# TensorE's program of a decode kernel: steps 16 to 127 as a hardware loop, with queries staged per group

## The chip, the cores and the metric

One core of one Trainium2 chip runs the kernel. The metric is the device time in microseconds (us) of one execution. A profiled execution gives a trace as well; its span is some 2 us shorter than the device time (1290.62 and 1292.84 us for the kernel before). Runs of one kernel agree within 0.7 us, so differences of 1 us can be told apart, although the verdict "same" covers everything within 2%. In the names of the profile PE is TensorE and PEld its weight loads, DVE is VectorE, ACT is ScalarE and SP is SyncE; a q behind a name stands for that engine's sequencer.

## The reference

A decode step for four sequences: layer norm, attention of one query token per sequence over a cache of 8192 keys and values in 32 heads, a residual, a second layer norm, a gated feed-forward block, a residual. Cut to what matters:

```python
B, Sq, D = 4, 1, 512
H, Sk, Dh = 32, 8192, 128
k_cache, v_cache: (B, H, Sk, Dh) bfloat16      # 268 MB each
q = (layernorm(x) @ wq) -> (B, H, 1, Dh)
p = softmax(q k^T * Dh**-0.5);  o = p v;  h = x + o @ wo
out = h + (sigmoid(g) * u) @ w_down,  g, u = layernorm(h) @ w_gate, w_up    # F = 1792
```

The caches are read once, and little is computed on each byte: the kernel is a stream out of HBM with some work alongside.

## The kernel before

A small scheduler collects the operations of every engine with their dependencies, counts semaphore values and writes each engine's program out in full. There are 128 steps, one per (sequence, head). K and V are loaded two heads at a time, 4 MB a load, into a ring of four slots. In each step DVE transposes the head's K in four pieces, TensorE computes 16 score matmuls, and ten steps later 16 matmuls with V. Softmax work is done per group of eight steps.

```python
GS, LAG, NS = 8, 10, 4                       # group size, lag of V behind K, ring slots

def emit(self, name, e):                     # one engine's program
    seen = {}
    for op in self.ops[name]:
        need = {}
        ...                                  # highest semaphore values that op's dependencies have
        for k, (v, s) in need.items():
            e.wait_ge(s, v)                  # a wait on a constant
            seen[k] = v
        ins = op.fn(e)
        if op.inc:
            ins.then_inc(op.sem, 1)
...
def dve_T(s):                                # K of step s, transposed by DVE in four pieces
    ...
    q = HT // 4
    for i in range(4):
        def f(e, i=i):
            return e.transpose(kT[:, buf, i * q:(i + 1) * q].bitcast(U32),
                               ringv(src)[:, base + i * q:base + (i + 1) * q].bitcast(U32))
        op = P("dve", f, [dma_of[it][0], sc_of.get(s - 2)])
        yield
...
def pe_score(s):                             # 16 matmuls; every step's queries have an address of their own
    t, u, g = s // 2, s % 2, s // GS
    hh = 4 * u + t % 4
    def f(e):
        mm = None
        for v in range(4):
            l0 = LQ0 + (t * 4 + v) * 32 - 4 * hh
            for j in range(4):
                rhs = ...
                mm = e.matmul(bS[g % 2][32 * j:32 * (j + 1), :], Lq[:, l0:l0 + 32], rhs, ...)
        return mm
```

The loads are issued by SyncE, each when its slot's last reader is done: a K slot after the DVE transposes, a V slot after the V matmuls on TensorE. After the last V come the weights of the output projection and of the feed-forward block (w_gate, w_up, then w_down in three pieces).

## Time and profile before

| | before |
|---|---|
| device time, median | 1293.15 us (1293.1 to 1293.17) |
| bytes from HBM | 550.77 MB, 427 GB/s over the span |
| data queue's share of the 16 DMA engines' time | 99.4% |
| busy: TensorE, DVE | 39%, 49% |
| instruction packets on queue 8 | 38, of 16 KB each |

From the page of the kernel before: the busy times; the span in 40 slices (DMA busy in tenths, and GB/s); the DMA queues (packets, MB, share of 16 engines); the chain that ended last, by engine and by line.

```profile
PE 499.5 (39%) x4851; PEld 189.0 (15%) x4851; DVE 637.6 (49%) x659; ACT 74.4 (6%) x134; POOL 10.6 (1%) x22
...
DMA  9999999999999999999999999999999999999997
GB/s 406 433 426 436 427 434 430 431 432 429 433 429 431 432 431 431 430 431 432 430 433 428 432 427 436 432 427 434 428 434 426 434 431 430 434 428 434 428 432 305
...
q1 hardware_dynamic: 20384, 550.78, 99.4%
q8 instruction: 38, 0.62, 0.2%
q14 instruction: 7, 0.06, 0.0%
...
DMA 85%; PE 12%; DVE 2%; issue 0%; SPq 0%; DVEq 0%
DMA ring<-in_A_v_cache_dram 78%; PE PS L436 7%; PE PS L412 4%; DMA ring<-in_B_w_up_dram 3%; DMA ring<-in_A_k_cache_dram 2%; DVE kT L394 1%; DMA ring<-in_A_wq_dram 1%; PE PS L467 0%; PE PS L323 0%; PE PS L631 0%; DVE Lq L367 0%; DVE ring L340 0%; PE PS L350 0%; PE PS L645 0%; DVE mx L450 0%
```

Every slice but the last has the DMA engines busy; the last one has the tail. Queue 1 carries the data, queues 8 and 14 carry instructions; the text calls the reading of one such instruction packet a fetch. No compute engine comes near full use, so outside the tail no saving of compute can pay directly.

The last pieces of the chain of waits, in order of time (start, duration, what):

```profile
1234.61 3.63 PE PS L436 x32
...
1238.68 43.65 DMA ring<-in_B_w_up_dram
...
1282.38 3.54 PE PS L631 x56
```

The kernel ends 8.28 us after the load of w_up lands at 1282.34 us. Whatever moves that landing moves the kernel.

Three rows of the timeline in the steady state (start, duration, engine, line, operation, in brackets what ended the idle time before it):

```profile
610.28 0.33 SPq L249 DMA_DIRECT2D ring<-in_A_k_cache_dram  x1
...
615.03 0.33 SPq L249 DMA_DIRECT2D ring<-in_A_v_cache_dram  x1
...
619.50 5.75 DVE L394 STREAM_TRANSPOSE kT<-ring 128x1024 uint32<-128x1024 uint32 x5 [2.70 <-DMA ring<-in_A_k_cache_dram]
```

A K slot is issued again at 610.3 us and a V slot at 615.0 us, while earlier loads are still to land.

One more reading was made from the trace. A load runs on 16 DMA engines, and each adds one to the load's semaphore when its share has landed (the trace has 16 such updates for each load). The 16 times of one load show how far the engines are apart. They are not labelled with the engine, so only their sorted order is known. For four loads (K loads except the last row; time of the first of the 16, then the sorted delays behind it, all in us):

```
before, first at    delays of the 16 shares
   90.0   0 .15 .23 .24 .28 .30 .34 .36 .37 .43 .50 .85 1.28 1.73 1.83 1.86
  478.6   0 .13 .19 .25 .38 .39 .82 1.55 1.77 2.10 3.22 3.33 3.35 3.37 3.39 3.90
  944.9   0 .06 .07 .26 .30 .61 .95 3.90 4.55 4.83 4.84 4.86 5.43 6.25 6.37 6.40
 1274.6   0 .01 .02 .16 .31 .51 .89 4.75 5.94 6.20 6.30 6.80 7.56 7.70 7.71 7.76   (w_up)
```

The fastest engine delivers a 4 MB load every 9.71 us from beginning to end. I call the last number of a row the lag.

### The profile page before, as it was taken

The numbers are of one execution on the slowest core, as the hardware profiler recorded it, in microseconds if no ns is written. First come the engines' busy times: TensorE is split into PE (matmuls) and PEld (weight loads), VectorE is DVE, ScalarE is ACT, GpSimd is POOL, SyncE is SP. The second block draws the span as 40 slices with busy tenths as digits, with TensorE's granted clock in tenths as the row PEclk, the third lists the DMA queues.
The fourth block names the chain that finished last, engine by engine and source line by source line (L and its number), as shares of the span: only waits on it lengthen the run. The fifth ranks groups of instructions, "written<-read, shape, count | busy, mean of one in ns | idle before, by whom it ended". The sixth has DMA issues, their size and how long they took to land.

```text
span 1290.6 us, 10784 instructions
## 1 busy us (share of the span) xinstructions
PE 499.5 (39%) x4851; PEld 189.0 (15%) x4851; DVE 637.6 (49%) x659; ACT 74.4 (6%) x134; POOL 10.6 (1%) x22
## 2 busy tenths in 40 slices
PE   2444334334234244333334343342343443443445
PEld 1011111111011011111111111110110111111114
DVE  5974644535545545535536445445445446355300
ACT  2010100001010010100101000010100101000011
POOL 3000000000000000000000000000000000000000
PEclk8556566565565665565665666665655656655665
DMA  9999999999999999999999999999999999999997
GB/s 406 433 426 436 427 434 430 431 432 429 433 429 431 432 431 431 430 431 432 430 433 428 432 427 436 432 427 434 428 434 426 434 431 430 434 428 434 428 432 305
DMA packets 20437, 551.46 MB, mean 427 GB/s; under 512 B 2212, under 2 KB 2216, under 8 KB 3624
## 3 DMA queue, kind: packets, MB, share of 16 engines
q1 hardware_dynamic: 20384, 550.78, 99.4%
q8 instruction: 38, 0.62, 0.2%
q14 instruction: 7, 0.06, 0.0%
q10 hardware_dynamic: 8, 0.00, 0.0%
HBM read 550.77 MB, written 0.00 MB: 427 GB/s over the span
## 4 chain that ended last, share of the span: by engine, by line
DMA 85%; PE 12%; DVE 2%; issue 0%; SPq 0%; DVEq 0%
DMA ring<-in_A_v_cache_dram 78%; PE PS L436 7%; PE PS L412 4%; DMA ring<-in_B_w_up_dram 3%; DMA ring<-in_A_k_cache_dram 2%; DVE kT L394 1%; DMA ring<-in_A_wq_dram 1%; PE PS L467 0%; PE PS L323 0%; PE PS L631 0%; DVE Lq L367 0%; DVE ring L340 0%; PE PS L350 0%; PE PS L645 0%; DVE mx L450 0%
## 5 line engine op out<-in xcount | busy, mean ns | idle before, releaser
L394 DVE STREAM_TRANSPOSE kT<-ring 128x1024 uint32<-128x1024 uint32 x512 | 588.1, 1209 | 480.7 <-DMA ring<-in_A_k_cache_dram 480.7
L412 PE MATMUL PS<-kT,Lq 128*32 128x512 bf16 x2048 | 242.7, 621 | 565.9 <-DVE kT L394 565.6
L436 PE MATMUL PS<-ring,PTz 128*32 128x512 bf16 x2048 | 216.6, 569 | 201.9 <-DMA ring<-in_A_v_cache_dram 201.9
L412 PEld LDWEIGHTS PS<-kT,Lq 128*32 128x32 bf16 x2048 | 70.2, 135 | 699.6 <-DVE kT L394 601.0
L436 PEld LDWEIGHTS PS<-ring,PTz 128*32 128x32 bf16 x2048 | 66.6, 128 | 320.0 <-DMA ring<-in_A_v_cache_dram 191.5
L497 DVE STREAM_TRANSPOSE Et<-Ep 128x512 bf16<-128x512 bf16 x16 | 11.4, 711 | 95.7 <-ACT Ep L493 95.7
L471 ACT ACTIVATE negm<-PS 128x1 f32<-128x1 f32 x16 | 2.7, 171 | 674.1 <-PE PS L467 674.1
L506 ACT ACTIVATE PTz<-Et 64x512 bf16<-64x512 bf16 x32 | 34.0, 1061 | 12.8 <-DVE Et L497 12.4
L534 ACT ACTIVATE A_sb<-PS 32x32 bf16<-32x32 f32 x16 | 3.8, 235 | 485.5 <-PE PS L532 485.5
L511 DVE TENSOR_SCALAR Zs<-PS,rinv 128x512 f32<-128x512 f32 x16 | 11.6, 723 | 27.7 <-PE PS L436 27.7
L518 PE MATMUL PS<-SelZ,Zs 128*128 128x8 f32 x128 | 18.4, 270 | 0.9 <-DVE Zs L511 0.9
L518 PEld LDWEIGHTS PS<-SelZ,Zs 128*128 128x128 f32 x128 | 16.9, 206 | 10.4 <-issue 8.6
L450 DVE TENSOR_REDUCE mx<-PS 128x1 f32<-128x512 f32 x16 | 10.5, 657 | 4.2 <-PE PS L412 4.1
L473 ACT ACTIVATE E_sb<-PS,negm 128x512 bf16<-128x512 f32 x16 | 11.0, 687 | 0.5
L493 ACT ACTIVATE Ep<-PS 128x512 bf16<-128x512 f32 x16 | 9.6, 597 | 10.4 <-PE PS L489 10.4
L478 PEld LDWEIGHTS PS<-sig,Gsum 128*128 128x128 f32 x32 | 7.8, 304 | 13.0 <-issue 13.0
L478 PE MATMUL PS<-sig,Gsum 128*128 128x1 f32 x32 | 9.2, 357 | 0.0
L467 PEld LDWEIGHTS PS<-onesf,rowx 1*128 1x128 f32 x32 | 6.6, 254 | 12.6 <-issue 12.6
L631 PE MATMUL PS<-hnT,ring 128*128 128x4 bf16 x112 | 7.0, 199 | 2.9 <-DMA ring<-in_B_w_gate_dram 2.0
L467 PE MATMUL PS<-onesf,rowx 1*128 1x1 f32 x32 | 7.9, 314 | 0.0
L524 DVE TENSOR_TENSOR OD<-PS,SelD 128x32 bf16<-128x32 f32 x16 | 2.5, 156 | 10.3 <-PE PS L518 10.3
L340 DVE CAST ring<-PS 128x512 bf16<-128x512 f32 x4 | 2.5, 682 | 10.0 <-PE PS L323 10.0
(85 smaller groups left out, 100.3 us busy)
## 6 DMA issues: line engine op xcount, KB each, us to landing
ring<-in_A_k_cache_dram SPq DMA_DIRECT2D x64, 4096.0 KB, 29.7
ring<-in_A_v_cache_dram SPq DMA_DIRECT2D x64, 4096.0 KB, 33.9
ring<-in_A_wq_dram SPq DMA_DIRECT2D x1, 4096.0 KB, 12.4
kT<-in_A_wo_dram SPq DMA_DIRECT2D x1, 2560.0 KB, 40.5
ring<-in_B_w_gate_dram SPq DMA_DIRECT2D x1, 1792.0 KB, 39.7
ring<-in_B_w_up_dram SPq DMA_DIRECT2D x1, 1792.0 KB, 43.7
kT<-in_A_wo_dram SPq DMA_DIRECT2D x1, 1536.0 KB, 43.7
ring<-in_B_w_down_dram SPq DMA_DIRECT2D x1, 896.0 KB, 37.2
```

The costliest lines, as they stand in the source:

```text
L394: return e.transpose(kT[:, buf, i * q:(i + 1) * q].bitcast(U32), ringv(src)[:, base + i * q:base + (i + 1) * q].bitcast(U32))
L412: mm = e.matmul(bS[g % 2][32 * j:32 * (j + 1), :], Lq[:, l0:l0 + 32], rhs, start=(s % GS == 0 and v == 0), stop=(s % GS == GS - 1 and v == 3),
L436: mm = e.matmul(bO[g % 2][32 * rq:32 * (rq + 1), :], PTz[:, g % 2, l0:l0 + 32], ringv(slot)[:, r0 * 128:(r0 + 4) * 128], start=(s % GS == ...
L450: mx_of[g] = P("dve", lambda e: e.tensor_reduce(mx[:, :], bS[g % 2][:, :], AX.X, ALU.max), [sc_of[g * GS + GS - 1], p1_of.get(g - 1)])
L467: p2_of[g] = P("pe", lambda e: e.matmul(bX[:, 0:1], rowx[0:1, :], onesf[0:1, 0:1], start=True, stop=True), [d2b_of[g], c_ones])
L473: exp_of[g] = P("act", lambda e: e.activation(E_sb[:, :], bS[g % 2][:, :], ACT.Exp, bias=negm[:, 0:1], scale=SCALE, accum_out=sig[:, 0:1]) ...
L478: L_of[g] = P("pe", lambda e: e.matmul(bX[:, 0:1], Gsum[:, :], sig[:, 0:1], start=True, stop=True), [exp_of[g], a1_of[g], d_g])
L493: epc_of[g] = P("act", lambda e: e.activation(Ep[:, :], bP[0][:, :], ACT.Copy), [pt_of[g], et_of.get(g - 1)])
L497: et_of[g] = P("dve", lambda e: e.transpose(Et[:, :], Ep[:, :]), [epc_of[g]] + list(ptc_of.get(g - 1, ())))
L506: return e.activation(dst, src, ACT.Copy)
L511: z_of[g] = P("dve", lambda e: e.tensor_scalar(Zs[:, :], bO[g % 2][:, :], rinv[:, g % 2:g % 2 + 1], None, op0=ALU.mult), [pv_of[g * GS + G ...
L518: mm = e.matmul(bP[1][:, 0:8], Zs[:, 128 * r:128 * (r + 1)], SelZ[:, r, :], start=(r == 0), stop=(r == 3))
```

## The change

TensorE's program for steps 16 to 127 becomes seven passes of a body of 16 steps. For this, everything that differed between passes has to become the same: ScalarE copies the queries of each group to a fixed address ahead of the group (`Lqg`), one product is put at a fixed PSUM row, waits compare with a register that is raised in each pass, and dummy operations make the counts of the first pass equal to those of the others. The evident intent is a smaller program; the arithmetic is the same. The diff, cut to its core:

```diff
+L0, LB = 16, 16
...
     def emit(self, name, e):
+        turns = self.turns(name) if name == "pe" else []
         for op in self.ops[name]:
+            if name == "pe" and op.turn is not None:
+                if op is turns[0][0]:
+                    self.emit_loop(name, e, turns, seen)
+                continue
...
+    def emit_loop(self, name, e, turns, seen):
+        ...
+        with e.Fori(0, len(turns)) as i:
+            for same, ds in zip(zip(*turns), fixed):
+                ...
+                    e.wait_ge(s, i * self.step[k] + base)
+                ins = same[0].fn(e)
+                if same[0].inc:
+                    ins.then_inc(same[0].sem, 1)
...
-        Lq = SB("Lq", [128, 32 + NT2 * 128], BF16)
+        Lq = SB("Lq", [128, NT2 * 16], BF16)
+        Lqg = SB("Lqg", [128, 2, LQ0 + 516], BF16)
...
+        def chain_lq(g):
+            lqg_of[g] = P("act", lambda e: e.activation(
+                Lqg[:, g % 2, LQ0:LQ0 + 512].rearrange("p (i a) -> p i a", a=32)[:, :, 0:4],
+                Lq[:, 64 * g:64 * g + 64].rearrange("p (i a) -> p i a", a=4), ACT.Copy),
+                [sc_of.get((g - 2) * GS + GS - 1), zlg] + ...)
...
-                    l0 = LQ0 + (t * 4 + v) * 32 - 4 * hh
+                    l0 = LQ0 + ((t % 4) * 4 + v) * 32 - 4 * hh
...
-            a_of[g] = P("pe", lambda e: e.matmul(bP[1][r0:r0 + 32, 16:48], OD[:, :], SelS[:, :], start=True, stop=True,
-                                                 tile_position=(0, r0)), [otc_of[g], d_sels, ac_of.get(g - 1)])
+            a_of[g] = P("pe", lambda e: e.matmul(bP[1][0:32, 16:48], OD[:, :], SelS[:, :], start=True, stop=True,
+                                                 tile_position=(0, 0)), [otc_of[g], d_sels, ac_of.get(g - 1)])
...
+        def blank(s, base, eng):             # dummy operations on ACT and DVE for equal counts
...
         for s in range(NST + LAG + 4):
+            prog.turn = (s - L0) // LB if L0 <= s < NST else None
```

More of the change, by code (lines that the diff above doesn't have):

```diff
@@ L17 @@
 NS = 4
+L0, LB = 16, 16
 class _Op:
-    __slots__ = ("eng", "fn", "deps", "inc", "val", "sem", "amount")
+    __slots__ = ("eng", "fn", "deps", "inc", "val", "sem", "turn")
     def __init__(self, eng, fn, deps):
@@ L36, in __init__ @@
         self.ops = {e: [] for e in self.ENGS}
+        self.turn = None
     def add(self, eng, fn, deps=(), sem=None, val=0):
@@ L40, in add @@
         op.sem, op.val = sem, val
+        op.turn = self.turn
         self.ops[eng].append(op)
@@ L49, in resolve @@
                         d.inc = True
+        self.step = {}
         for e in self.ENGS:
+            turns = self.turns(e)
+            for same in zip(*turns):
+                if any(op.inc for op in same):
+                    for op in same:
+                        op.inc = True
             n = 0
@@ L55, in resolve, with turns, needs @@
                     op.sem, op.val = sems[e], n
+            if turns:
+                assert len({len(t) for t in turns}) == 1
+                self.step[id(sems[e])] = sum(op.inc for op in turns[0])
+    def turns(self, e):
+        by = {}
+        for op in self.ops[e]:
+            if op.turn is not None:
+                by.setdefault(op.turn, []).append(op)
+        return [by[k] for k in sorted(by)]
+    @staticmethod
+    def needs(name, op, but=()):
+        need = {}
+        for d in op.deps:
+            if d in but or d.eng == name == "pe":
+                continue
+            k = id(d.sem)
+            if d.val > need.get(k, (0, None))[0]:
+                need[k] = (d.val, d.sem)
+        return need
     def emit(self, name, e):
         seen = {}
+        turns = self.turns(name) if name == "pe" else []
         for op in self.ops[name]:
-            need = {}
-            for d in op.deps:
-                if d.eng == name == "pe":
-                    continue
-                k = id(d.sem)
-                if d.val > seen.get(k, 0) and d.val > need.get(k, (0, None))[0]:
-                    need[k] = (d.val, d.sem)
-            for k, (v, s) in need.items():
-                e.wait_ge(s, v)
-                seen[k] = v
+            if name == "pe" and op.turn is not None:
+                if op is turns[0][0]:
+                    self.emit_loop(name, e, turns, seen)
+                continue
+            for k, (v, s) in self.needs(name, op).items():
+                if v > seen.get(k, 0):
+                    e.wait_ge(s, v)
+                    seen[k] = v
             ins = op.fn(e)
@@ L72, in emit @@
                 ins.then_inc(op.sem, 1)
+    def emit_loop(self, name, e, turns, seen):
+        first = {}
+        fixed = [set(same[0].deps).intersection(*(op.deps for op in same[1:])) for same in zip(*turns)]
+        for op, ds in zip(turns[0], fixed):
+            for k, (v, s) in self.needs(name, op, set(op.deps) - ds).items():
+                if v > seen.get(k, 0):
+                    e.wait_ge(s, v)
+                    seen[k] = v
+        with e.Fori(0, len(turns)) as i:
+            for same, ds in zip(zip(*turns), fixed):
+                need = [self.needs(name, op, ds) for op in same]
+                for k in sorted({k for n in need for k in n}, key=lambda k: [k in n for n in need]):
+                    vals = [(t, n[k][0]) for t, n in enumerate(need) if k in n]
+                    s = next(n[k][1] for n in need if k in n)
+                    if k not in self.step:
+                        self.step[k] = (vals[-1][1] - vals[0][1]) // (vals[-1][0] - vals[0][0])
+                    base = {v - t * self.step[k] for t, v in vals}
+                    assert len(base) == 1, (vals, self.step[k])
+                    base = base.pop()
+                    if k in first and base <= first[k]:
+                        continue
+                    first[k] = base
+                    e.wait_ge(s, i * self.step[k] + base)
+                ins = same[0].fn(e)
+                if same[0].inc:
+                    ins.then_inc(same[0].sem, 1)
+        for k, base in first.items():
+            seen[k] = base + (len(turns) - 1) * self.step[k]
 def bass_sequential_preLN__mha_block_cached__glu_gated_glu__decode_kernel(
@@ L133, in bass_sequential_preLN__mha_block_cached__glu_gated_glu__decode_kernel @@
         lnst = SB("lnst", [128, 16], FP32)
+        blk = SB("blk", [128, 4], FP32)
         xT = SB("xT", [128, NDC * B], FP32)
@@ L267, in bass_sequential_preLN__mha_block_cached__glu_gated_glu__decode_kernel @@
         zlq = pool(lambda e: e.memset(Lq[:, :].bitcast(FP32), 0.0))
+        zlg = pool(lambda e: e.memset(Lqg[:, :, :].rearrange("p b f -> p (b f)").bitcast(FP32), 0.0))
         zs = pool(lambda e: e.memset(Sel[:, :, :], 0.0))
@@ L361, in f @@
                     ps = slice(32 * a, 32 * a + 32)
-                    dst = Lq[ps, LQ0 + b * H2 * 128 + a:LQ0 + b * H2 * 128 + a + (H2 * 4 - 1) * 32 + 1:32].rearrange(
-                        "p (h v) -> p h v", v=4)
+                    dst = Lq[ps, b * H2 * 16 + a:(b + 1) * H2 * 16:4].rearrange("p (h v) -> p h v", v=4)
                     src = bX[ps, :].rearrange("p (h e v b) -> p e h v b", e=2, v=4, b=4)[:, a // 2, :, :, b]
@@ L380, in bass_sequential_preLN__mha_block_cached__glu_gated_glu__decode_kernel @@
                                                     AX.X, ALU.add), [c_selz4])
-        T_of, sc_of, pv_of = {}, {}, {}
+        T_of, sc_of, pv_of, lqg_of = {}, {}, {}, {}
         mx_of, d2_of, exp_of, pt_of, ptc_of, L_of, d3_of = {}, {}, {}, {}, {}, {}, {}
@@ L399, in dve_T @@
             consumed[it] = op
+        def chain_lq(g):
+            lqg_of[g] = P("act", lambda e: e.activation(
+                Lqg[:, g % 2, LQ0:LQ0 + 512].rearrange("p (i a) -> p i a", a=32)[:, :, 0:4],
+                Lq[:, 64 * g:64 * g + 64].rearrange("p (i a) -> p i a", a=4), ACT.Copy),
+                [sc_of.get((g - 2) * GS + GS - 1), zlg] + ([o for ops in lq_of for o in ops] if g == 0 else []))
         def pe_score(s):
@@ L411, in f @@
                                       [[2 * HT, 128], [128, 16], [2, 32]])
-                        mm = e.matmul(bS[g % 2][32 * j:32 * (j + 1), :], Lq[:, l0:l0 + 32], rhs,
+                        mm = e.matmul(bS[g % 2][32 * j:32 * (j + 1), :], Lqg[:, g % 2, l0:l0 + 32], rhs,
                                       start=(s % GS == 0 and v == 0), stop=(s % GS == GS - 1 and v == 3),
@@ L417, in pe_score @@
             if s % GS == 0:
-                deps.append(exp_of.get(g - 2))
-            if s % H == 0:
-                deps += lq_of[s // H]
+                deps += [exp_of.get(g - 2), lqg_of[g]]
             if s == 0:
@@ L531, in chain_a @@
             r0 = 32 * (g % 4)
-            a_of[g] = P("pe", lambda e: e.matmul(bP[1][r0:r0 + 32, 16:48], OD[:, :], SelS[:, :], start=True, stop=True,
-                                                 tile_position=(0, r0)), [otc_of[g], d_sels, ac_of.get(g - 1)])
-            ac_of[g] = P("act", lambda e: e.activation(A_sb[r0:r0 + 32, :, g // 4], bP[1][r0:r0 + 32, 16:48], ACT.Copy),
+            a_of[g] = P("pe", lambda e: e.matmul(bP[1][0:32, 16:48], OD[:, :], SelS[:, :], start=True, stop=True,
+                                                 tile_position=(0, 0)), [otc_of[g], d_sels, ac_of.get(g - 1)])
+            ac_of[g] = P("act", lambda e: e.activation(A_sb[r0:r0 + 32, :, g // 4], bP[1][0:32, 16:48], ACT.Copy),
                          [a_of[g]])
@@ L539, in hook, with f @@
             return g if (s - base) % GS == 0 and 0 <= g < NG else None
+        def blank(s, base, eng):
+            if (s - base) % GS == 0 and L0 - GS <= s < L0:
+                def f(e):
+                    if eng == "act":
+                        return e.activation(blk[0:B, 0:1], lnst[0:B, 0:1], ACT.Copy)
+                    return e.tensor_copy(blk[0:B, base - 18:base - 17], lnst[0:B, 0:1])
+                P(eng, f, [d_a]).inc = True
         for s in range(NST + LAG + 4):
+            prog.turn = (s - L0) // LB if L0 <= s < NST else None
+            g = hook(s, 0)
+            if g is not None:
+                chain_lq(g)
             g = hook(s, 10)
@@ L562, in bass_sequential_preLN__mha_block_cached__glu_gated_glu__decode_kernel @@
                 chain_z(g)
+            else:
+                blank(s, 19, "dve")
             g = hook(s, 20)
@@ L565, in bass_sequential_preLN__mha_block_cached__glu_gated_glu__decode_kernel @@
                 chain_otc(g)
+            else:
+                blank(s, 20, "dve")
             if s < NST:
@@ L588, in bass_sequential_preLN__mha_block_cached__glu_gated_glu__decode_kernel @@
                 chain_a(g)
+            else:
+                blank(s, 20, "act")
+        prog.turn = None
         gl = NG - 1
```

## The prediction

> **What bounds the kernel now.** DMA bandwidth. The page gives 427 GB/s, the engines busy at 9 tenths or more in all slices but the last, queue 1 with 99.4% of their time; the chain that ended last is 85% DMA. PE is busy 39%, DVE 49%. The landings of the K and V loads, read engine by engine from the trace, show more: the fastest DMA engine lands its share of a 4 MB load every 9.714 us from beginning to end, while half of the engines fall behind it, by 1.9 us at 100 us and 7.8 us at the end. The slowest one closes the last weight load (chain: w_up lands at 1282.3 us), and 8.3 us of PE and DVE work follow.
>
> **Where the lag comes from.** Queue 8 (instruction) moved 38 packets of 16 KB, one per about 256 PE instructions (4851 matmuls, as many weight loads), and beside each a data packet takes 1.7 us in place of 1.215. Their durations repeat with period 8, so I take eight engines to serve them in turn. Four or five fetches each and a lag of 6.0 to 7.8 us make about 1.5 us per fetch on its engine (an estimate from these numbers).
>
> **What the change does.** PE work is the same: 32 matmuls a step. Removed: most of PE's static instructions. Added: register arithmetic and a separate wait per changing dependency (some 50 in a body), seven passes with a jump back, a ScalarE copy of 128x64 per group (about 0.2 us; the 128x512 copy took 0.6), three dummy operations. Steps 16 to 127 take about 1100 us, a pass 157 us; PE needs about half of it.
>
> **On the critical path: almost none.** In the steady state (timeline at 600 us) a K slot is reissued at 610.3 and a V slot at 615.0, while loads already issued keep the engines busy to about 629 and 639 us: PE may be 19 to 24 us late before DMA starves. [...] Prologue: step 0 now waits for all query copies, but DVE does these before the first K transpose anyway.
>
> **What remains is fetch traffic.** The body is about 1,100 matmuls and weight loads and 100 to 150 others: five blocks of 256. [...] If the body stays resident: about 16 fetches, two per engine, lag about 3.5 us, time about 1289. If fetched on each pass: 46 to 60 fetches, lag 9 to 12 us if in turn, more if the same engines serve the same blocks: 1294 to 1300. The second seems somewhat likelier.
>
> **Predicted: 1293.5 us, 8 in 10 between 1288.5 and 1299.** Faster by over 2%: 0.01; within 2%: 0.97; slower by over 2%: 0.02.
>
> **What would show it.** Queue 1 still over 99%; slices flat near 430 GB/s; the chain still V loads, then w_up; PE busy about 500 us, with more issue gaps; queue 8 packets near 16 or near 50; the slowest engine's lag at the end near 3.5 us or over 8 us, and the time moving with it; the same 8.3 us tail.
>
> **What would make it wrong.** A jump back that stalls PE over 20 us (fetches queue behind data packets), so that slots come free late: dips in GB/s every 157 us, K transposes waiting for matmuls. Register waits so costly that PE nears 9.7 us a step. Fetches falling on one engine: lag of tens of us. Or the lag not coming from fetches: then the time does not move.

The jump back and the register waits were counted as absorbed in the 19 to 24 us. Neither was a term of the sum: about 1289 us if the body stays (if it is not fetched again on later passes) and 1294 to 1300 us, 1297 in the middle, if it is fetched on each pass. Evenly weighed these make 1293 us; with the slight lean to the second, 1293.5 us.

## More of the kernel before

The waits, as total, times and longest of each pair:

```profile
PEld PS L412 <- DVE kT L394: 601.0, 69, 11.1
...
DVE kT L394 <- DMA ring<-in_A_k_cache_dram: 480.7, 59, 11.3
...
PEld PS L412 <- issue: 97.4, 368, 0.3
```

DVE waits for the K loads and TensorE waits for DVE: everybody waits for the stream.

## The result, and the profile after

The changed kernel takes 1289.74 us (median of 6 runs, 1289.6 to 1289.94) against 1293.12 us (median of 6, 1292.79 to 1293.21). The ratio is 0.9974, with a 95% interval of 0.9961 to 0.9987: 3.4 us less, small but clear of noise. Ratios here are the mean time of one kernel's runs over that of the other's of the same rounds, so they are not quite the ratios of the medians quoted.

The same lines of the page after:

```profile
PE 496.7 (39%) x4851; PEld 187.4 (15%) x4851; DVE 638.2 (50%) x661; ACT 77.3 (6%) x151; POOL 8.1 (1%) x23
...
DMA  9999999999999999999999999999999999999997
GB/s 407 431 430 431 431 430 432 429 432 428 436 431 431 431 432 433 430 434 430 434 429 435 430 433 429 434 429 435 428 436 427 436 427 436 428 435 429 434 429 311
...
q1 hardware_dynamic: 20384, 550.78, 99.5%
q8 instruction: 12, 0.20, 0.1%
q14 instruction: 7, 0.06, 0.0%
...
DMA 85%; PE 12%; DVE 2%; issue 0%; SPq 0%; DVEq 0%
DMA ring<-in_A_v_cache_dram 79%; PE PS L504 7%; PE PS L482 4%; DMA ring<-in_B_w_up_dram 3%; DMA ring<-in_A_k_cache_dram 2%; DVE kT L457 1%; DMA ring<-in_A_wq_dram 1%; PE PS L535 0%; PE PS L387 0%; PE PS L720 0%; DVE Lq L430 0%; DVE ring L404 0%; PE PS L414 0%; PE PS L734 0%; DVE mx L518 0%
```

TensorE does the same 4851 matmuls. Queue 8 moved 12 packets in place of 38. The GB/s slices rise by less than one per cent, which is hard to see there. The end of the chain of waits:

```profile
1232.03 3.63 PE PS L504 x24
...
1236.10 43.66 DMA ring<-in_B_w_up_dram
...
1279.81 3.54 PE PS L720 x56
```

The tail behind the landing of w_up is as long as before, 8.28 us; the landing itself is at 1279.77 us, 2.57 us earlier. (The two spans differ by 2.6 us, the two medians by 3.4: the profiled runs took 1292.84 and 1289.94 us, at the near ends of the two ranges.) The timeline shows the stream's cycle unchanged:

```profile
608.81 0.33 SPq L312 DMA_DIRECT2D ring<-in_A_k_cache_dram  x1
...
613.26 0.33 SPq L312 DMA_DIRECT2D ring<-in_A_v_cache_dram  x1
...
618.06 8.00 DVE L457 STREAM_TRANSPOSE kT<-ring 128x1024 uint32<-128x1024 uint32 x7 [2.96 <-DMA ring<-in_A_k_cache_dram]
```

The V slot is issued again 4.45 us after the K slot, in place of 4.75 us. The waits show one trap:

```profile
DVE kT L457 <- DMA ring<-in_A_k_cache_dram: 478.3, 61, 11.3
PEld PS L482 <- DVE kT L457: 449.4, 54, 10.8
PEld PS L482 <- issue: 239.9, 372, 11.2
```

Weight loads for the scores wait 152 us less for DVE and 143 us more for "issue". TensorE was not slowed by that. Register instructions now stand ahead of some of these weight loads, and the profile books the same waiting under another name; the sum is 698 us before and 689 us after.

What the loop costs is in the trace's records of TensorE's register and branch instructions, which are not counted as busy: 210 register operations of 32 ns, 21 fused ones of 37 to 50 ns, and seven branches (236, 213, 207, 207, 207, 208 and, not taken, 76 ns). That is about 1.3 us per pass of 155 us, in which the matmuls are busy for 58.9 us (38%; the prediction estimated about half of a pass). The ScalarE copies of the queries take 0.24 to 0.26 us each (estimated: 0.2). There is no separate wait instruction for each register wait: TensorE has 29 stand-alone semaphore instructions, and had 28 before.

The landings, as above:

```
after, first at     delays of the 16 shares
   90.2   0 .08 .10 .14 .16 .17 .20 .25 .31 .48 .50 .59 1.36 1.68 1.97 2.01
  478.7   0 .09 .11 .50 .52 .56 .57 1.62 1.63 1.68 1.69 1.76 1.81 1.95 2.00 2.30
  944.9   0 .17 .18 .59 .66 .67 1.37 1.75 1.79 1.85 1.86 1.89 1.92 2.09 2.11 4.37
 1274.5   0 .16 .23 .62 .69 .75 1.42 1.76 1.79 1.85 1.87 1.94 3.42 3.62 3.64 5.26   (w_up)
```

The fastest engine lands w_up at the same time as before (1274.51 and 1274.58 us). Through the loop most of the others stop falling back. The lag at w_up is 5.26 us in place of 7.76 us: 2.50 of the 2.57 us. But one engine still falls back alone.

### The profile page after: what moved, and what is told of

Same layout as the page of the kernel before. It is cut to its first block, busy times and chain, and to the rows that moved or that the text cites. A ratio compares the mean times of both kernels' runs of the same rounds, so it can differ in the third digit from the quotient of the medians.

```text
span 1288.0 us, 11045 instructions
## 1 busy us (share of the span) xinstructions
PE 496.7 (39%) x4851; PEld 187.4 (15%) x4851; DVE 638.2 (50%) x661; ACT 77.3 (6%) x151; POOL 8.1 (1%) x23
## 4 chain that ended last, share of the span: by engine, by line
DMA 85%; PE 12%; DVE 2%; issue 0%; SPq 0%; DVEq 0%
DMA ring<-in_A_v_cache_dram 79%; PE PS L504 7%; PE PS L482 4%; DMA ring<-in_B_w_up_dram 3%; DMA ring<-in_A_k_cache_dram 2%; DVE kT L457 1%; DMA ring<-in_A_wq_dram 1%; PE PS L535 0%; PE PS L387 0%; PE PS L720 0%; DVE Lq L430 0%; DVE ring L404 0%; PE PS L414 0%; PE PS L734 0%; DVE mx L518 0%
## 5 line engine op out<-in xcount | busy, mean ns | idle before, releaser
L482 PE MATMUL PS<-kT,Lqg 128*32 128x512 bf16 x2048 | 241.7, 619 | 566.8 <-DVE kT L457 560.3
L482 PEld LDWEIGHTS PS<-kT,Lqg 128*32 128x32 bf16 x2048 | 69.6, 135 | 697.2 <-DVE kT L457 449.4
L579 DVE TENSOR_SCALAR Zs<-PS,rinv 128x512 f32<-128x512 f32 x16 | 11.6, 723 | 27.1 <-PE PS L504 27.1
L720 PEld LDWEIGHTS PS<-hnT,ring 128*128 128x128 bf16 x112 | 6.9, 161 | 3.1 <-DVE hnT L711 2.2
L557 PE MATMUL PS<-E_sb,Sel 128*32 128x512 bf16 x64 | 6.5, 400 | 1.9 <-ACT E_sb L541 1.1
```

What stands on the lines that cost most here:

```text
L482: mm = e.matmul(bS[g % 2][32 * j:32 * (j + 1), :], Lqg[:, g % 2, l0:l0 + 32], rhs, start=(s % GS == 0 and v == 0), stop=(s % GS == GS - 1 ...
L579: z_of[g] = P("dve", lambda e: e.tensor_scalar(Zs[:, :], bO[g % 2][:, :], rinv[:, g % 2:g % 2 + 1], None, op0=ALU.mult), [pv_of[g * GS + G ...
L720: mm = e.matmul(bk[:, B * t:B * t + B], wv[:, c, t:F:NFT], hnT[:, B * c:B * c + B], start=(c == 0), stop=(c == NDC - 1))
```

## The experiments

The theory (F): an instruction packet delays the DMA engine that carries it, delays pile up because that engine never catches up in a stream without gaps, and the kernel ends when the slowest engine has landed w_up. The loop's body stays, that is, it is not fetched again (in after no packet of queue 8 moves between 263.3 and 1225.8 us, while TensorE works off 6989 instructions), so there are fewer packets. Rivals: the other edits made the gain (S); TensorE's load matters rather than the packets (P); any loop would do (L). Each kernel was timed against the kernel before on the same chip.

One slip in the expectations has to be told. The lags that they quote for after and before "at the last w_up load" were read at neighbouring loads: 7.84 and 5.40 us are those of w_gate, 5.16 us that of the last piece of w_down. At w_up they are 7.76 and 5.26 us. All measured lags below are at w_up.

### e1: the change without the loop

```diff
-            if name == "pe" and op.turn is not None:
+            if False:
```

> The changed kernel with everything but the loop: queries staged per group, dummy operations, fixed PSUM row for the last product, but TensorE's program written out. Theory F (the gain is instruction fetch traffic: in the trace of before 38 packets of 16 KB, in the trace of after 12, and the lag of the slowest DMA engine behind the fastest at the last w_up load is 7.84 us before and 5.40 us after): 38 fetches again, lag 7 to 8.5 us, time 1292.5 to 1293.8, so the gain of 3.4 us is gone. Rival S (the gain comes from the shorter prologue memset, the staged queries or the other small edits): time stays at 1289.5 to 1290.3.

Measured: 1292.82 us (1292.78 to 1292.95), ratio to before 0.9998 (0.9985 to 1.0012), lag 8.02 us.

The page has 38 packets on queue 8, as before:

```profile
q8 instruction: 38, 0.62, 0.2%
```

All of the packets and all of the time are back. The staging, the shorter clearing of memory and the other edits give at most 0.3 us. Rival S falls.

### e2: a body of 32 steps

```diff
-L0, LB = 16, 16
+L0, LB = 32, 32
```

> The same loop with a body of 32 steps from step 32 on (three passes). The body is about 2300 instructions[...]. Theory F with residency: the body does not stay and is fetched again on each pass, 36 to 45 fetches, lag 7 to 9 us, time 1292.5 to 1294.5; the jump back takes microseconds instead of the 0.2 us of after. Rival L (any loop saves, as the code is smaller): fetches near 20, time below 1291. Rival S: 1289.7, whatever the fetches.

That this body would not stay was a supposition, which this run tests.

Measured: 1294.47 us (1294.31 to 1294.48), ratio 1.001 (0.9996 to 1.0024), 43 packets, lag 9.53 us (half a microsecond above the range expected for it). One pass is 2262 TensorE instructions by the trace, against 1132 in the change. The two taken branches last 6.51 and 6.60 us in place of 0.21 us. A loop whose body does not stay gains nothing: rival L falls. The long branch costs nothing by itself, though. The first one begins at 592.77 us and ends at 599.28 us. From the timeline of that stretch:

```profile
594.78 0.16 PEld L504 LDWEIGHTS PS<-ring,PTz 128*32 128x32 bf16 x4 [0.27 <-issue]
...
600.24 4.62 DVE L457 STREAM_TRANSPOSE kT<-ring 128x1024 uint32<-128x1024 uint32 x4 [10.30 <-DMA ring<-in_A_k_cache_dram]
...
604.99 0.14 PEld L482 LDWEIGHTS PS<-kT,Lqg 128*32 128x32 bf16 x8 [10.05 <-issue]
```

The weight loads ahead of the jump had been queued when it began and end at 594.94 us, and TensorE's next scores could not begin before the K that DVE received at 600.24 us had been transposed. The branch lies inside that wait. The fastest engine lands w_up at 1274.54 us, as in before.

### e3 and e4: more TensorE instructions, written out and in the loop

Both get 16 tiny matmuls (one column, result never read) in every step. e3 is e1 with them, e4 the changed kernel with them.

```diff
             def f(e):
                 mm = None
+                for _ in range(16):
+                    e.matmul(bH[0:32, 256:257], ident[:, 0:32], ident[:, 0:1], start=True, stop=True,
+                             tile_position=(0, 0))
                 for v in range(4):
```

> The written-out program of e1 with 16 tiny matmuls more in each step (32 instructions, results never read), so 4096 more TensorE instructions and some 16 more fetches: 54. Theory F: two more fetches on each of eight DMA engines at about 1.4 to 1.5 us, lag 10 to 11 us, time e1 plus 2.5 to 3.5 us, 1295.5 to 1297. Rival P (TensorE's extra work costs the time, not the fetch): the same plus should then show in the loop with the same work (e4). Rival S: no change from e1, as TensorE has slack.

> The loop of the changed kernel with the same 16 tiny matmuls in each step: TensorE executes as many instructions as in e3, but the body is about 1670 instructions[...]. Theory F: 14 to 17 fetches, lag 5.3 to 6.5 us, time 1289.7 to 1290.8, 5 to 7 us below e3. Rival P: the same rise over the changed kernel as e3 over e1, so about 1293.

The second expectation said that the body should stay, which its number of fetches supposes; until then only the body of 1132 instructions had been seen to.

Measured: e3 1295.75 us (1295.62 to 1295.92), 54 packets, lag 11.01 us; e4 1289.7 us (1289.62 to 1289.79), 16 packets, lag 5.08 us, ratios to before 1.0021 (1.0007 to 1.0034) and 0.9974 (0.996 to 0.9988). Busy times and instruction queue of e3:

```profile
PE 550.0 (43%) x6899; PEld 254.3 (20%) x6899; DVE 638.3 (49%) x661; ACT 77.3 (6%) x151; POOL 8.1 (1%) x23
...
q8 instruction: 54, 0.88, 0.3%
```

and of e4:

```profile
PE 553.4 (43%) x6899; PEld 255.3 (20%) x6899; DVE 635.5 (49%) x661; ACT 77.4 (6%) x151; POOL 8.3 (1%) x23
...
q8 instruction: 16, 0.26, 0.1%
```

TensorE is about equally busy in both, over 50 us more than in after. Written out, the extra instructions cost 2.9 us; in the loop they cost nothing. So it is the fetching and not the executing that is paid for: rival P falls. A body of 1644 instructions stays: 16 packets in place of 54.

### e5, e8, e6 and e7: whose engine is the last one now?

In after, one engine is 1.6 us behind the next. The lag grows by about 1 us (0.98 to 0.99 us by the records of the packets, see below) when an 8 KB packet of queue 14 moves: such packets begin at 55, 278, 511, 746 and 992 us, and DVE works off 123 to 130 instructions between each two. (Two more, at 305 and 729 us, do not fit DVE's count. By the counts the first goes with ScalarE, which has worked off 63 instructions at that packet in before and 60 in after, and the second with SyncE, which has worked off 79 in both; the records do not name the engine served.) So DVE's instruction count was changed, by cutting K's transpose into other pieces: one, two or eight a step in place of four.

```diff
+NTR = 1                                    # e5, e7; 2 in e8, 8 in e6
-            q = HT // 4
+            q = HT // NTR
-            for i in range(4):
+            for i in range(NTR):
...
-            for i in range(4):
+            for i in range(NTR):
                 next(tr, None)
-                if i == 1:
+                if i == (NTR - 1) // 2:
```

> The changed kernel with one 128x4096 K transpose a step on DVE in place of four 128x1024 (128 instructions in place of 512). In after a single DMA engine is the slowest, 5.16 us behind at the last w_up load; its lag grows by about 1 us at the times of 8 KB instruction packets on queue 14, which come every 220 to 250 us, as often as DVE works off some 128 instructions. Theory F2 (that engine serves DVE's fetches, and it sets the end now): 2 or 3 such packets of DVE in place of 5, its lag 2 to 3.3 us, the slowest engine now one that serves TensorE's fetches at 3.3 to 3.7 us, time 1287.8 to 1288.6. Rival O (the last engine is slow for another reason, and DVE's instructions do not matter): 1289.7, lag 5.2.

> The changed kernel with two 128x2048 K transposes a step (256 instructions). Theory F2: 3 or 4 fetches of DVE, lag of its engine 3 to 4 us, time 1287.9 to 1288.9, between e5 and after. Rival O: 1289.7.

> The changed kernel with eight 128x512 K transposes a step on DVE (1024 instructions). DVE has room: it is 50% busy. Theory F2: 9 or 10 fetches of DVE, lag of its DMA engine 8.5 to 10 us, the others unchanged (3.5 us and less), time 1293 to 1294.8. Rival O: 1289.7; a rival in which DVE's longer work delays slots would show as the fastest engine's last landing moving from 1278.9 us.

> The kernel before with one K transpose a step. Theory F2 with the slowest engine deciding: in before the eight engines that serve TensorE's fetches lag 5.8 to 8.25 us and DVE's about 4.6 us, so that taking DVE's fetches away gains nothing: 1292.7 to 1293.3, lag 7.6 to 8.3. Rival Q (fetches cost by their sum, or cheaper DVE work helps by itself): the same gain as e5 over the changed kernel, about 1.5 us, so 1291.5.

| kernel | K transposes a step | time, us | ratio to before (95%) | lag, us | next slowest, us |
|---|---|---|---|---|---|
| after | 4 | 1289.74 | 0.9974 (0.9961 to 0.9987) | 5.26 | 3.64 |
| e5 | 1 | 1288.32 | 0.9963 (0.9949 to 0.9977) | 3.47 | 3.42 |
| e8 | 2 | 1288.43 | 0.9964 (0.995 to 0.9977) | 3.65 | 3.48 |
| e6 | 8 | 1293.55 | 1.0003 (0.999 to 1.0017) | 8.61 | 3.26 |
| e7 (from before) | 1 | 1293.1 | 1.0 (0.9986 to 1.0013) | 8.16 | 8.02 |

The page of e5:

```profile
PE 499.1 (39%) x4851; PEld 189.1 (15%) x4851; DVE 614.7 (48%) x277; ACT 77.4 (6%) x151; POOL 8.1 (1%) x23
...
q8 instruction: 12, 0.20, 0.1%
q14 instruction: 4, 0.03, 0.0%
```

The page of e6:

```profile
PE 499.3 (39%) x4851; PEld 188.3 (15%) x4851; DVE 668.4 (52%) x1173; ACT 77.4 (6%) x151; POOL 8.1 (1%) x23
...
q8 instruction: 12, 0.20, 0.1%
q14 instruction: 11, 0.09, 0.0%
```

In e6 nine packets of queue 14 fit DVE's count, and one engine alone is 8.6 us late while the next is at 3.3 us: all of the loop's gain is lost again through DVE. In e5 the last engine is level with the next ones. e7 makes the rule plain: there the same DVE saving brings nothing, because TensorE's packets keep other engines at 8 us. The slowest engine decides, not the sum. That DVE also saves 23 us of busy time in e5 and e7 does not show in the time of e7. Rivals O and Q fall. e5 beats both kernels, by 4.8 us against before and 1.4 us against after; e8 is level with it. (After was timed in another round. The kernel before reads 1293.12 us in that round and 1293.1 us in this one, and no run of e5, at most 1288.51 us, reaches the fastest run of after, 1289.6 us.)

### e9 and e10: TensorE late once per pass

The changed kernel with 120 (e9) or 320 (e10) of the tiny matmuls ahead of the scores of the body's first step.

```diff
+                for _ in range(120 if s % LB == 0 and L0 <= s else 0):      # 320 in e10
+                    e.matmul(bH[0:32, 256:257], ident[:, 0:32], ident[:, 0:1], ...)
```

> The changed kernel with 120 tiny matmuls ahead of the scores of the first step of each pass, so that TensorE is late once per pass. At 107 ns per matmul with its weight load, as the trace of after shows for the scores (four in 0.427 us), that is up to 13 us. The theory that loads already issued cover a lateness of 19 to 24 us (reissue of slots against landings in the timeline): no starvation, fastest engine's last landing still 1278.8 to 1279.1 us, time 1289.5 to 1291. Rival T (there is little slack, so that a late TensorE costs its lateness): seven times several us, 1310 and more.

> The same with 320 tiny matmuls, up to 34 us late, the body still about 1770 instructions. Slack of 19 to 24 us: each of the six or seven late passes starves DMA for 5 to 15 us, the fastest engine's last landing moves by 40 to 100 us, time 1330 to 1390, with slices of lower GB/s. If the time stays below 1295 the slack is larger than I read; if e9 is already slow it is smaller.

Measured: e9 1289.67 us (1289.58 to 1290.01), ratio 0.9974 (0.9957 to 0.9992); e10 1298.89 us (1298.44 to 1299.11), ratio 1.0045 (1.0027 to 1.0063). The time of e9 is as expected, and its fastest engine lands w_up at 1274.40 us: nothing starves, and rival T falls for a lateness of this size. The time of e10 is far below the expected 1330 to 1390 us. Both expectations about the size of the stall missed: the 120 matmuls took 3.3 us in the trace and the 320 took 10.6 to 11.2 us, as a tiny matmul was issued every 27 ns and not every 107 ns. In e10 each group of 320 also holds one gap of 2.1 to 2.7 us, and an instruction packet moves in each of the seven gaps, so that TensorE seems to have waited there for its next instructions. And e10 is no clean test, because its body of 1772 instructions no longer stayed: 69 packets, and taken branches of 6.4 to 6.9 us. So its TensorE was late by more than the 11 us.

```profile
GB/s 404 435 430 427 434 431 426 435 428 427 433 429 433 427 423 430 431 433 431 418 433 435 426 429 425 430 432 432 420 428 429 429 433 409 431 435 428 431 432 313
...
q8 instruction: 69, 1.13, 0.4%
...
DMA 70%; DVE 19%; PE 9%; issue 3%; SPq 0%; DVEq 0%
```

It is nevertheless the one run in which the stream has holes. Slices of 409, 418 and 420 GB/s stand in the list, DVE's share of the chain that ended last is 19% in place of 2%, and the fastest engine lands w_up at 1282.34 us, 7.8 us later than in the other runs. The holes can be foreseen from a simple measure: the time from the issue of a load until the fastest engine has landed the load before it, in which that engine still has work. Its smallest values over the steady part are 11.7 us in before, 11.6 us (13.3 us within the loop) in after, 10.8 us in e9 and −1.0 us in e10; where it falls to about zero in e10, the fastest engine's step between two loads is up to 12.4 us in place of 9.7. In e11 and e12 below it is 5.2 and 3.8 us, still without a hole. So TensorE has about 12 us to spare at the tightest slots, if its lateness delays the issue one for one; that is an estimate, and no run tests it cleanly.

### e11 and e12: how large may the body be?

The changed kernel with 22 (e11) and 28 (e12) tiny matmuls in each step, otherwise as e4.

> The changed kernel with 22 tiny matmuls in each step: by the trace 1132 instructions in a pass of after and 1644 with 16, so 1836 here[...]. [...]15 to 18 fetches, jump back 0.2 us, 1289.5 to 1290.8. [...]fetched again, 60 and more fetches, lag 11 us and more, time above 1295.

> The same with 28 tiny matmuls in a step: 2028 instructions in a pass[...]. I expect that it does not stay: 55 to 70 fetches, jump back of 3 us and more, lag 11 to 14 us, time 1295.5 to 1299. If it stays: 1289.5 to 1291 and about 18 fetches.

In both expectations a comparison of the body with a limit is cut, in the first also the conditions of its two outcomes, since no run had shown what they say. The first reads: if the body stays, 15 to 18 fetches and 1289.5 to 1290.8 us; if it does not, 60 and more fetches and above 1295 us.

Measured: e11 1298.83 us (1298.77 to 1299.18), ratio 1.0045 (1.0027 to 1.0063), 72 packets, lag 14.26 us; e12 1300.29 us (1300.18 to 1300.38), ratio 1.0055 (1.0037 to 1.0073), 79 packets, lag 15.65 us. Taken branches last 5.9 to 7.1 us. The pages of e11 and e12:

```profile
q8 instruction: 72, 1.18, 0.4%
...
q8 instruction: 79, 1.29, 0.4%
```

So neither 1836 nor 2028 instructions stay; for e11 this was the second of the two outcomes that I had left open, for e12 the expected one, at a time above its range. Together with e4 (1644, stays), e9 (1372, stays) and e10 (1772, does not stay) the limit lies between 1644 and 1772 instructions of a pass in these programs. A taken branch lasted 0.21 to 0.24 us in the passes that stayed and 5.9 to 7.1 us in those that did not.

### All runs in one sum

The span is the time at which the fastest engine lands w_up, plus the lag, plus the tail behind it:

| kernel | queue 8 packets | fastest lands w_up, us | lag, us | tail, us | span, us |
|---|---|---|---|---|---|
| before | 38 | 1274.58 | 7.76 | 8.28 | 1290.62 |
| e1 | 38 | 1274.57 | 8.02 | 8.29 | 1290.88 |
| e2 | 43 | 1274.54 | 9.53 | 8.27 | 1292.34 |
| e3 | 54 | 1274.54 | 11.01 | 8.30 | 1293.86 |
| e11 | 72 | 1274.40 | 14.26 | 8.29 | 1296.95 |
| e12 | 79 | 1274.53 | 15.65 | 8.31 | 1298.48 |
| after | 12 | 1274.51 | 5.26 | 8.28 | 1288.04 |
| e4 | 16 | 1274.40 | 5.08 | 8.28 | 1287.76 |
| e5 | 12 | 1274.63 | 3.47 | 8.29 | 1286.38 |
| e6 | 12 | 1274.76 | 8.61 | 8.28 | 1291.65 |
| e7 (from before) | 38 | 1274.54 | 8.16 | 8.27 | 1290.97 |
| e8 | 12 | 1274.64 | 3.65 | 8.30 | 1286.59 |
| e9 | 13 | 1274.40 | 5.00 | 8.29 | 1287.69 |
| e10 | 69 | 1282.34 | 5.90 | 8.29 | 1296.54 |

The first and the last term are constants except in e10, whose holes let the late engines catch up. From before to e12 the packets grow by 41, about five on each of eight engines, and the lag by 7.89 us: 1.54 us per packet on its engine.

The records of the single packets show where this time goes. A data packet of 32 KB takes about 1.22 us and begins as another ends, so that the packets of one engine can be followed. (Each of the 35 instruction packets named below begins within 0.004 us of the end of a data packet.) In before one of them ends at 593.21 us; an instruction packet of 16 KB runs from 593.20 to 594.27 us; the next data packet begins at 594.26 us and takes 1.71 us. So the data are held up by 1.05 us, while the instruction packet has the engine, and then by another 0.49 us: 1.54 us together. For all 35 packets of queue 8 in before between 20 and 1250 us, the length of the packet and the excess of the data packet behind it make 1.47 to 1.58 us, with a median of 1.57. For the five 8 KB packets in after that fit DVE's count they make 0.98 to 0.99 us (0.33 and 0.66). Lags can be counted in this way: five packets of 1.57 us make 7.8 us (before: 7.76), ten make 15.7 us (e12: 15.65), nine of 0.98 us make 8.8 us (e6: 8.61).

## Why the prediction was right or wrong

The measured 1289.74 us lies inside the range of 1288.5 to 1299 and in the class given 0.97. The central value of 1293.5 us had the wrong sign: it forecast a change within noise, and there was a gain of 3.4 us. That the range held was in part luck: it was wide enough to hold both outcomes, and the one that was called likelier did not come.

- **DMA bandwidth bounds the kernel, and the slowest engine's lag sets its end.** Right, and shown by e3, e6 and the sum over all runs.
- **"About 1.5 us per fetch on its engine", eight engines in turn.** Right in size: 1.54 us from the lags, 1.57 us from the packets themselves. That there are eight is inferred: durations repeat with period 8 (in before 1.018, 1.018, 1.081, 1.068, 1.060, 1.098, 1.108 and 1.086 us for the packets from 809 us on, then 1.016, 1.018, 1.081, 1.069, 1.061 and 1.108 us), and in e11 just eight engines lag by 12.4 to 14.3 us (a ninth, presumably DVE's, by 5.1 us). The records do not name the engine.
- **"The second seems somewhat likelier"** (the body fetched again on each pass). This is the step that failed, and it set the central value. The body of 1132 instructions stays: 12 packets, branches of 0.21 us. What the runs show is a limit of size: bodies of 1132 to 1644 instructions stay (12 to 16 packets), bodies of 1772 and more do not (69 to 79 packets; 43 in the three passes of e2).
- **"If the body stays resident: about 16 fetches, two per engine, lag about 3.5 us, time about 1289".** Nearly right: 12 fetches, 5.26 us, 1289.74 us. The mis-sized term is the lag. TensorE's engines came to 3.6 us as estimated. The engine that carries DVE's fetches had not been considered. In before it is hidden behind the others: presumably the lone 4.75 us of the last row, since e7 has 2.13 us in that place. e5 shows the estimate's 3.5 us once it is out of the way.
- **If fetched again: "46 to 60 fetches, lag 9 to 12 us", "1294 to 1300".** e2, a real loop that does not stay, has 43 fetches, 9.53 us and 1294.47 us. Its jumps back took 6.51 and 6.60 us, and were absorbed. But its passes are three of 2262 instructions; a body of 16 steps without padding that is fetched in each pass was not among the runs.
- **"A separate wait per changing dependency (some 50 in a body)".** Too much. There are 30 register operations and three fused ones in a pass and no added wait instructions to speak of, 1.3 us a pass with the branch.
- **"PE may be 19 to 24 us late before DMA starves".** Too much. I had measured against the landing of a whole load, which is the slowest engine's. The fastest engine runs out first, and it has 11.7 us at the tightest slot. The conclusion that the loop's cost is absorbed held.
- **Tail of 8.3 us, TensorE's busy time, the chain.** Unchanged, as predicted.

What stays open: why a 16 KB instruction packet takes 1.07 us, when a data packet of 32 KB takes 1.22 us; why the data packet behind an instruction packet takes longer; and what sets the limit between 1644 and 1772 instructions.

## What to carry to other kernels

In this kernel, which streams without a gap, a DMA engine that was delayed did not catch up: in before the slowest was 1.86 us behind at 90 us and 7.76 us at the end. (Only in e10, with its holes, was the lag as small as 5.90 us in spite of 69 packets.) In a kernel like it, look at the landings of the single engines and not only at their mean: the slowest decides. Instructions are then traffic too: fewer instructions on an otherwise idle engine (a loop whose body is not fetched again, 3.4 us here, or larger pieces per instruction, another 1.4 us in e5) can pay although the stream does not wait for that engine (the fastest DMA engine lands w_up at 1274.58 us in before and at 1274.51 us in after), and a body slightly too large loses more than the loop gained: e11, with 1836 instructions in a pass, took 9.1 us longer than e4 with 1644. When one cause is removed, look for the next engine behind it before summing up further gains.
